# k'v of two batches in spare PSUM columns, ups in halves, w_v in longer runs and a new order of steps, in an attention and channel-mix kernel

## The chip, the cores and the metric

The kernel runs on one core of a Trainium2 chip. The metric is the device time of one execution in microseconds; of several executions the median is given. The core has five engines that run their own instruction streams and wait for each other through semaphores: PE (TensorE, matrix products), DVE (VectorE), ACT (ScalarE), POOL (GpSimd) and SP (SyncE, which here only issues transfers). PE multiplies out of SBUF and writes into PSUM, which has eight banks of 512 fp32 columns on each of 128 partitions. DVE and ACT read PSUM and write SBUF.

## The reference

Eight batches of attention with separate normalisations of q and k, and then a channel mix on its output:

```
q_s = softmax of q over the head dimension;  k_s = softmax of k over the sequence
kv  = k_s^T v   (64 x 64 for each head);      x = q_s kv          # q, k, v: (8, 8, 576, 64)
x:  (8, 8, 576, 64) -> (8, 576, 512)
xk  = mu_k * x + (1 - mu_k) * x_prev;         xr = mu_r * x + (1 - mu_r) * x_prev
out = sigmoid(xr @ w_r) * ((relu(xk @ w_k) ** 2) @ w_v)
```

x_prev is x moved by one position of the sequence, with zeros at the front. The width is 512, the hidden width F is 1024, the sequence 576. Inputs and output are float32; the products are taken in bf16.

## The kernel before, in words

All weights are cast to bf16 and stay in SBUF. The eight batches go through two stages. The attention stage works on halves of a batch (u = 0, 1: four heads each) and leaves the mixed inputs xk and xr of the batch, transposed (512 channels on partitions, 576 positions along the free dimension). The channel-mix stage takes xk by batch and xr by pairs of batches.

**Attention of a half.** `exp` on ACT makes eq and ek out of the loaded q and k. `cast_v` makes vb, whose last column of each head is 1, so that the product with it also gives the column sums. `sum_q` and `scale_q` on DVE normalise q into qs. For the first two batches (NM = 2, the "mixed" ones) `turn_q` transposes qs on PE into a pair of PSUM banks and two `evict_q` copy it to qT, 320 columns from one bank and 256 from the other (in the profile: qT, 128x640 and 128x512 bf16); later batches use a DMA transpose. `kv` is 36 small matmuls, 65 columns wide, into both banks of a pair. After it come, for the later batches, `norm_kv` and `x`, and then the mix from x on ACT and DVE (`shift_x`, `mix_x`). For the two mixed batches `weigh_kv` folds mu into kv instead: for w = 0 (mu_k) a reciprocal and two multiplications, for w = 1 (mu_r) two more, all on DVE, all reading kv in PSUM. Then `x_mixed` takes kvm and qT to xk (w = 0) or xr (w = 1) in two parts, c = 0 (320 positions, 12 matmuls) and c = 1 (256 positions, 8 matmuls), each into its own pair of banks, and `evict_mixed` on ACT or DVE copies each to SBUF.

**Channel mix.** `up(b, f)` is one of the eight tiles of F of one batch: 16 matmuls in two groups (a = 0, 1), 288 positions each, into the two banks of a pair. `relu` on ACT evicts the pair, `square` (DVE or ACT) squares two tiles at once into k2. `gate` (four matmuls), `tanh`, `down` (eight matmuls), `finish` and `store` make 128 rows of output. Gates and downs use single banks.

**PSUM.** Six banks are three pairs, two0 to two2; two are single, one0 and one1. A step that needs a pair takes the one that the plan frees first.

**Order.** `Plan.run` goes through the table ORDER, a list of step numbers with a letter where a step may go to one of several engines (A ACT, D DVE, G POOL). It gives each step a planned start from written costs (`T_NARROW`, `TURN` and the numbers in each `pl.step`), and picks buffers by it. `emit` sorts all steps by planned start and calls them in this order. So ORDER and the costs fix the order of instructions on each engine's queue, and on each queue of transfers, but not the waits: these come from the layer that builds the program, which orders a step behind the steps emitted earlier that touch the same buffers. Every engine runs its queue in order.

**Weights.** w_k comes in two transfers of 1 MB (columns 0 to 511, then 512 to 1023 of F) and is cast in eight steps of 128 columns of F; w_v comes in two transfers of 1 MB, 512 rows each, and is cast in four. Row 128 f + p of w_v lands on partition p, so a partition receives four runs of 2 KB for each transfer.

**Start.** While PE waits in the first microseconds, extra matmuls on an identity (`warm`) are put into planned gaps, up to the start of the step `up(0, 0)`.

In the profile the lines that matter below are L332 (`exp`), L342, L344 and L347 (`sum_q`, `scale_q`), L361 (`turn_q`), L378 (`kv`), L391 and L393 (`weigh_kv`), L410 (`x_mixed`), L454 (`up`), L459 (`relu`), L473 (`gate`), L490 (`down`), L320 (`warm`), and the copies, which all have the line of the helper: L237 on ACT, L238 on DVE and POOL.

Of the kernel before, what the change touches and what calls it, by code (L numbers as in the profile page):

```python
# [20 lines left out]
ORDER = """  # L21
7 0 2 8 1 76 3 80 81 4 9 10 96 11 5 100 78G 77 79A 82 85 83A 12 6 13 84A 97 14 101 86 87 28 102
103A 90 92 91A 104D 93A 98G 99G 19 105 94 95A 16G 88 17G 106 107 108 89A 27 109D 24 110 111A 29
23G 136 15A 114 18D 112 362 363 21G 115D 367 30 113D 31 365 360 22G 25 32 368 26 33 372 20A 37
34 40 366 361 377 375 140 141 116 378 364D 376 370 120 371 369D 121 142 119G 526 536 117 527
143D 138G 122 42 373 118D 537 39G 144D 124D 125 43 137 521 531 123D 139A 44 38G 126 127 130 131A
128 129A 145 146 147 134 41 135A 148 149A 532 150 151D 36G 374A 152 154 153D 385 387 155D 35D
386 382 397 522 379D 156 159 388 523 398 160 389A 158 524 528 380 173 176 177 174 46 161 529 383
381 45 157 390 391 178 530 538 190 539 395 162 132 533 396 163 399A 392 133A 164 393 561 193 166
534 165 384D 47 49 394D 562 541 48 175 167 168 542 169 179 55 180 551 50 546 194 195 552 535 181  # L30
170 547 186 187 172 171 188 182 51 563 183 564 548 556 184 207 412 413 191 192 185 210 417 189
402 418 403 415 410 540 211 241 565 405 209 416 549 411 407 212 208 419D 408 406 244 245 576 196
197 400 56 57 557 571 401 414D 577 213 198 409D 572 200 404D 214 558 199 202 203 201 543 215 559
544 204 206 205 52 216 581 566 582 217 219 53 54 567 220 221 224 218 225 525 222 227 223 568 578
427 432 428 242 550 569 430 243 431 433 420 421 247 226 230 434A 586 246 437 228 248 438 587 579
422 423 58 231 249 254 255 424D 256 59 229 570 583 250 257 560 251 584 545 553 258 253 232 554
61 237 66 252 234 573 574 233 591 64 238 425 606 236 60 426 259 235 63 239 260 435 240 277 261
65 607 452 436 442 447 439D 429D 596 453 262 592 443 440 575 448 275 445 294 450 292 446 278 608
62 279 580 441 295 449D 451 597 293 263 455 264 280 298 598 444A 454A 609 601 299 456 276 265
599 266 600 602 267 268 281 282 270 555 611 612 67 588 269 68 272 621 283 589 271 274 622 273  # L40
285 284 593 73 289 594 69 626 286 610 288 627 457 616 458 603 459A 296 290 287 343 309 460 74
291 467 461 468 462 463 346 465 311 470 472 466 297 312 477 310 313 471 344 75 604 469D 590 628
478 345 473 300 585 314 617 347 71 315 618 302 595 629 316 641 301 305 619 304 464A 306 475 308
646 642 647 630 613 476 307 303 348 474A 317 323 479D 322 349 614 350 620 636 637 319 638 643
324 318 320 485 321 487 488 72 328 644 651 325 652 486 70 497 639 640 498 489D 492 326 329 490
493 327 495 496 482 483 330 491 499D 623 351 332 357 624 661 353 615 653 333 480 356 662 331
494D 481 358 654 352 656 657 631 632 359 484D 334 625 633 340 335 336 355 673 655 339 634 648
337 354 341 517 342 518 338 505 649 666 510 645 650 667 704 671 506 705 511 672 507 681 674 706
707 682 512 635 500 508 509A 513 515 675 676 514D 658 659 677 516 502 501 503 504D 660 519D 668
669 605 670 663 664 665 683 684 678 679 691 685 686 692 696 687 688 697 680 708 520 689 690 701  # L50
702 693 694 703 695 698 699 700
"""


class Plan:
# [6 lines left out]

    TURN = 0.2

# [78 lines left out]
def kernel(  # L143
# [28 lines left out]


    const = ctx.enter_context(tc.tile_pool(name="const", bufs=1))
    psum = ctx.enter_context(tc.tile_pool(name="psum", bufs=1, space=bass.MemoryType.PSUM))
# [110 lines left out]
    def wk_raw():  # L286
        return f32(at("k2", "w"), CT * F).rearrange("p (c a f) -> p a c f", a=2, c=CT)
# [80 lines left out]
    def dma_turn_q(b, u):  # L368
        nc.sync.dma_start_transpose(out=at("qT", b, u)[:],
                                    in_=at("qs", b, u)[:].rearrange("p j c -> p (j c)"))  # L370

    def kv(b, u):
        ps, ek, vb = at("two", "kv", b, u), at("ek", b, u), at("vb", b, u)
        for j in range(J):
            for g in range(2):
                for h in range(2):
                    r = slice(64 * g, 64 * g + 64)
                    nc.tensor.matmul(ps[64 * h:64 * h + 64, g, 0:65],  # L378
                                     lhsT=ek[r, j, 64 * h:64 * h + 64], rhs=vb[r, j, h, :],
                                     start=(j == 0), stop=(j == J - 1))  # L380

    def norm_kv(b, u):
        ps, rz = at("two", "kv", b, u), inv_k(b, u)
        nc.vector.reciprocal(out=rz, in_=ps[:, :, 64])
        nc.vector.tensor_tensor(out=at("kvs", b, u)[:], in0=ps[:, :, 0:64],
                                in1=rz[:, :, None].to_broadcast((128, 2, 64)), op=ALU.mult)

    def weigh_kv(b, u, w):
        ps, rz, rows = at("two", "kv", b, u), inv_k(b, u), slice(2 * w, 2 * w + 2)
        if w == 0:  # L390
# [147 lines left out]

    T_UP, T_GATE, T_DOWN, T_NARROW = 0.98, 0.863, 1.725, 0.5

# [41 lines left out]
    for a in range(2):  # L582
        first.append(dma(2.75, lambda a=a: load_wv(a), uses=[sl("k2", "w")],
                         after=[*queue, *(ev["wk", i] for i in range(FT))]))
# [4 lines left out]
    for b in range(2, B):  # L589
        for u in range(2):  # L590
            for n in "qkv":
                ld(n, b, u, first)

    for n in range(B):
        for u in range(2):
# [26 lines left out]
            s = sl("two", "kv", n, u)  # L622
            p = pl.step("PE", T_NARROW, lambda n=n, u=u: kv(n, u), after=[ke, *vc],
                        uses=[ek, vb, s], lat=0.3, narrow=True)
            if n < NM:
                km = sl("kvm", n, u)
                nk = [p, ev["mu"]]
                for w in range(2):
                    nk.append(pl.step("DVE", 0.75 - 0.2 * w, lambda n=n, u=u, w=w: weigh_kv(n, u, w),
                                      after=nk, uses=[s, km, sl("mub")], lat=0.18))  # L630
                for w in range(2):
                    for c in range(2):
                        s = sl("two", "xm", n, u, w, c)
                        p = pl.step("PE", 0.47 if c == 0 else 0.41,
                                    lambda n=n, u=u, w=w, c=c: x_mixed(n, u, w, c),
# [24 lines left out]
    for b in range(B):  # L660
        mixed = [ev["mix", b, u, 0, c] for u in range(2) for c in range(2)]
        relus = []
        for f in range(FT):
            s, r = sl("two", "up", b, f), sl("rel", b, f // 2)
            ev["up", b, f] = pl.step("PE", T_UP, lambda b=b, f=f: up(b, f),
                                     after=[ev["wk", f], *mixed], uses=[sl("xk", b), s], lat=0.2)
            relus.append(pl.step("ACT", 0.54, lambda b=b, f=f: relu(b, f),
                                 after=[ev["up", b, f]], uses=[s, r], lat=0.2))
            if f % 2:
# [5 lines left out]
    for s in (ev["prep"], ev["up", 0, 0]):  # L675
        pl.link(s, [], [sl("one", "warm")])
    branch = pl.step("PE", 0.3, lambda: part())
    branch["tail"] = "first"
    for i in range(B // 2):
        for m in range(J):  # L680
# [3 lines left out]
                        after=[*ev["wr"], *(ev["mix", b, u, 1, c] for b in bs for u in range(2)  # L684
                                            for c in range(2))],
                        uses=[sl("xr", i), s, th], lat=0.2)
# [146 lines left out]
```

## Time and profile before

| what | value |
|---|---|
| median of 3 runs | 199.26 us (199.06 to 199.76) |
| the profiled execution's own time | 199.28 us |
| its span, first to last instruction | 197.5 us |
| mean granted clock of PE | 0.989 |
| matmuls of up, gate, down (busy) | 66.8, 35.8, 66.2 us |
| DMA | 46.86 MB, mean 237 GB/s over the span |

The span is what the profile's lines cover; about 1.8 us of the time lie around it. In the page, a first part gives the busy time of each engine. A second divides the span into 40 slices of about 4.9 us, with one digit each for the busy tenths; PEclk is the clock that PE was granted, 9 being full. A timeline line gives the start, the time of the group, the engine, the line, the operation, the output and inputs, how many instructions are merged, and in brackets the idle time before it with what ended it. A line of the windows gives a stretch, its length, the busy time (and count) of PE, of PE's weight loads, DVE, ACT and POOL, then PE's granted clock, the DMA's busy share and GB/s.

### The profile page before, as it was taken

The numbers are of one execution on the slowest core, as the hardware profiler recorded it, in microseconds if no ns is written. First come the engines' busy times: TensorE is split into PE (matmuls) and PEld (weight loads), VectorE is DVE, ScalarE is ACT, GpSimd is POOL, SyncE is SP. The second block draws the span as 40 slices with busy tenths as digits, with TensorE's granted clock in tenths as the row PEclk, the third lists the DMA queues.
The fourth block names the chain that finished last, engine by engine and source line by source line (L and its number), as shares of the span: only waits on it lengthen the run. The fifth ranks groups of instructions, "written<-read, shape, count | busy, mean of one in ns | idle before, by whom it ended". The sixth has DMA issues, their size and how long they took to land. (4 is left out here: it accounts for less than half of the span.)

```text
span 197.5 us, 4726 instructions
## 1 busy us (share of the span) xinstructions
PE 186.5 (94%) x1903; PEld 111.4 (56%) x1903; DVE 145.6 (74%) x225; ACT 144.7 (73%) x212; POOL 30.4 (15%) x42
## 2 busy tenths in 40 slices
PE   6699899899999999999998999999999999999991
PEld 4366665655547754664675545755476546664441
DVE  1979896797899799948999779887658859126222
ACT  3898688799797986989769988998749591671210
POOL 2042763420120222000080000230200000000000
PEclk9879999999999999999999999999999999999998
DMA  5999999989999999869993499999622540515634
GB/s 207 371 399 386 389 390 386 389 314 240 276 388 205 229 397 294 272 61 278 403 399 87 86 250 359 318 229 276 236 51 59 113 106 10 124 30 124 162 72 127
DMA packets 35896, 46.86 MB, mean 237 GB/s; under 512 B 16280, under 2 KB 16544, under 8 KB 35872
## 3 DMA queue, kind: packets, MB, share of 16 engines
q1 hardware_dynamic: 35456, 46.02, 77.7%
q10 hardware_dynamic: 416, 0.53, 1.0%
q8 instruction: 15, 0.25, 0.5%
q14 instruction: 9, 0.07, 0.1%
HBM read 33.56 MB, written 9.44 MB: 218 GB/s over the span
## 5 line engine op out<-in xcount | busy, mean ns | idle before, releaser
L454 PE MATMUL two<-xk,wk_bf 128*128 128x288 bf16 x512 | 66.8, 286 | 1.2 <-POOL wk_bf L238 0.9
L490 PE MATMUL one<-wv_bf,k 128*128 128x512 bf16 (+1 forms) x296 | 66.2, 374 | 0.1
L454 PEld LDWEIGHTS <-wk_bf 128*128 128x128 bf16 x512 | 49.8, 98 | 18.1 <-POOL wk_bf L238 1.2
L459 ACT ACTIVATE rel<-two 128x576 bf16<-128x576 f32 x64 | 39.9, 650 | 20.3 <-PE two L454 17.0
L490 PEld LDWEIGHTS <-k 128*128 128x128 bf16 x296 | 28.1, 98 | 31.2 <-issue 0.8
L473 PE MATMUL one<-wr_bf,xr 128*128 128x512 bf16 x144 | 35.8, 379 | 0.0
L238 POOL CAST vb<-ldv 128x1152 bf16<-128x1152 f32 (+1 forms) x17 | 19.2, 1132 | 102.0 <-DMA ldv<-in_v_dram 94.0
L440 ACT ACTIVATE aw<-two,om 128x575 bf16<-128x575 f32 x48 | 32.6, 752 | 2.5 <-PE two L432 2.5
L478 ACT ACTIVATE th<-one 128x512 f32<-128x512 f32 x36 | 21.4, 603 | 13.5 <-PE one L473 13.4
L496 DVE SCALAR_TENSOR_TENSOR ot<-th,one 128x512 f32<-128x512 f32 x33 | 22.4, 681 | 11.9 <-PE one L490 9.1
L469 DVE TENSOR_TENSOR k<-rel 128x1152 bf16<-128x1152 bf16 x22 | 18.6, 860 | 11.3 <-ACT rel L459 11.2
L342 DVE TENSOR_REDUCE rs<-eq 128x18 f32<-128x1152 bf16 x16 | 21.6, 1348 | 3.4 <-ACT eq L332 3.3
L347 DVE TENSOR_TENSOR qs<-eq,inv 128x1152 bf16<-128x1152 bf16 x16 | 23.7, 1484 | 0.3
L445 DVE SCALAR_TENSOR_TENSOR xk<-two,mu,aw 128x576 bf16<-128x576 f32 x24 | 19.1, 812 | 3.3 <-ACT aw L440 3.3
L332 ACT ACTIVATE eq<-ldq 128x1152 bf16<-128x1152 f32 x16 | 18.5, 1170 | 3.2 <-DMA ldq<-in_q_dram 3.0
L473 PEld LDWEIGHTS <-xr 128*128 128x128 bf16 x144 | 13.4, 98 | 13.1 <-issue 0.2
L445 DVE SCALAR_TENSOR_TENSOR xr<-two,mu,aw 128x576 bf16<-128x576 f32 x24 | 19.1, 803 | 1.1 <-ACT aw L440 1.0
L332 ACT ACTIVATE ek<-ldk 128x1152 bf16<-128x1152 f32 x16 | 18.7, 1171 | 0.5 <-DMA ldk<-in_k_dram 0.5
L467 ACT ACTIVATE k<-rel 128x1152 bf16<-128x1152 bf16 x10 | 11.6, 1171 | 0.2
L378 PE MATMUL two<-vb,ek 64*64 64x65 bf16 x576 | 7.9, 197 | 1.0 <-ACT ek L332 0.5
L378 PEld LDWEIGHTS <-ek 64*64 64x64 bf16 x576 | 6.4, 110 | 3.9 <-ACT ek L332 0.9
L320 PE MATMUL one<-ident 128*128 128x256 bf16 x29 | 6.6, 387 | 1.8 <-DVE halves L258 1.8
(56 smaller groups left out, 86.0 us busy)
## 6 DMA issues: line engine op xcount, KB each, us to landing
ldq<-in_q_dram SPq DMA_DIRECT2D x16, 576.0 KB, 5.9
ldk<-in_k_dram SPq DMA_DIRECT2D x16, 576.0 KB, 8.4
out_dram<-ot SPq DMA_DIRECT2D x66, 128.0 KB, 2.5
ldv<-in_v_dram SPq DMA_DIRECT2D x14, 576.0 KB, 7.7
k<-in_moe_w_k_dram SPq DMA_DIRECT2D x2, 1024.0 KB, 12.6
k<-in_moe_w_v_dram SPq DMA_DIRECT2D x2, 1024.0 KB, 11.0
ldv<-in_v_dram SPq DMA_DIRECT2D x4, 288.0 KB, 10.5
xr<-in_moe_w_r_dram SPq DMA_DIRECT2D x1, 1024.0 KB, 13.1
```

The lines of the kernel that those rows point to most:

```text
L238: return {"DVE": nc.vector, "POOL": nc.gpsimd}[eng].tensor_copy(out=out, in_=in_)
L332: nc.scalar.activation(out=at("e" + n, b, u)[:].rearrange("p j (h d) -> p h j d", h=2), in_=at("ld" + n, b, u)[:].rearrange("p h (j d) -> ...
L342: nc.vector.reduce_sum(out=rs[:], in_=at("eq", b, u)[:].rearrange("p j (h d) -> p (j h) d", h=2), axis=AX.X)
L347: nc.vector.tensor_tensor(out=at("qs", b, u)[:].rearrange("p j (h d) -> p (j h) d", h=2), in0=at("eq", b, u)[:].rearrange("p j (h d) -> p ...
L440: nc.scalar.activation(out=at("aw", b, u, h, w)[:, 1:S], in_=x_of(b, u, h)[:, 1:S], func=ACT.Copy, scale=om[:, c:c + 1])
L445: nc.vector.scalar_tensor_tensor(out=blend(b, w)[:, 2 * u + h, :], in0=x_of(b, u, h)[:, 64:64 + S], scalar=mu[:, c:c + 1], in1=at("aw", b, ...
L454: nc.tensor.matmul(ps[:, a, 0:HS], lhsT=wk_bf[:, ct, 128 * f:128 * f + 128], rhs=xk[:, ct, HS * a:HS * a + HS], start=(ct == 0), stop=(ct ...
L459: nc.scalar.activation(out=at("rel", b, f // 2)[:, f % 2, :].rearrange("p (a c) -> p a c", a=2), in_=at("two", "up", b, f)[:, :, 0:HS], fu ...
L473: nc.tensor.matmul(at("one", "rp", i, m)[:], lhsT=at("xr", i)[:, ct, 128 * m:128 * m + 128], rhs=wr_bf[:, ct, :], start=(ct == 0), stop=(c ...
L478: nc.scalar.activation(out=at("th", i, m)[:], in_=at("one", "rp", i, m)[:], func=ACT.Tanh, scale=0.5)
L490: nc.tensor.matmul(at("one", "vp", i, m, a)[:, cols], lhsT=at("k2", i)[:, f, 128 * m:128 * m + 128], rhs=wv_bf[:, f, cols], start=(f == 0) ...
L496: nc.vector.scalar_tensor_tensor(out=at(kept(i, m), i, m)[:, cols], in0=at("th", i, m)[:, cols], scalar=1.0, in1=at("one", "vp", i, m, a)[ ...
```

## The change

The new home of kv for the mixed batches is a third kind of buffer, "spare", which is not new memory: it is columns 320 to 384 of both banks of two1 and two2.

```diff
+    bufs["spare"] = [t[:, :, 320:385] for t in bufs["two"][1:]]
...
+    def kv_of(b, u):
+        if b < NM:
+            return at("spare", "kv", b, u)
+        return at("two", "kv", b, u)[:, :, 0:65]
...
-        ps, ek, vb = at("two", "kv", b, u), at("ek", b, u), at("vb", b, u)
+        ps, ek, vb = kv_of(b, u), at("ek", b, u), at("vb", b, u)
```

`norm_kv` and `weigh_kv` read through `kv_of` as well, and the plan takes a "spare" for these kv instead of a pair. Because `x` writes across columns 320 to 384 of a pair, it gets the weighings of the mixed batches as predecessors in the plan:

```diff
+                weighed += nk[2:]
...
-            p = pl.step("PE", T_NARROW, lambda n=n, u=u: x(n, u), after=[nk, *T],
+            p = pl.step("PE", T_NARROW, lambda n=n, u=u: x(n, u), after=[nk, *T, *weighed],
```

The ups of the two mixed batches become two steps each, one for each group of eight matmuls; the first half needs only the c = 0 parts of xk. A gate needs only the parts of xr whose positions it reads.

```diff
-    def up(b, f):
+    def up(b, f, parts=(0, 1)):
...
-        for a in range(2):
+        for a in parts:
...
+            for a in ((0, 1),) if b >= NM else ((0,), (1,)):
+                ev["up", b, f] = pl.step(
+                    "PE", T_UP * len(a) / 2, lambda b=b, f=f, a=a: up(b, f, a),
+                    after=[ev["wk", f], *(ev["mix", b, u, 0, c] for u in range(2)
+                                          for c in range(2) if c in a or c == 0 or b >= NM)],
+                    uses=[sl("xk", b), s], lat=0.2)
```

w_v is read so that partition p gets rows 4p to 4p + 3 of each half, one run of 8 KB. The order of F within a half changes with it, and the casts of w_k follow: each takes every fourth column of its half, a read stride of four fp32.

```diff
-            ap=[[C, 128], [128 * C, 4], [1, C]]))
+            ap=[[4 * C, 128], [1, 4 * C]]))
...
-        a, c = f // 4, 128 * (f % 4)
-        copy(eng, wk_bf[:, :, 128 * f:128 * f + 128], wk_raw()[:, a, :, c:c + 128])
+        units = wk_raw()[:, f // 4, :, :].rearrange("p c (e i) -> p c i e", i=4)
+        copy(eng, wk_bf[:, :, 128 * f:128 * f + 128], units[:, :, f % 4, :])
```

Written costs change (T_NARROW 0.5 to 0.55, TURN 0.2 to 0.25, `x_mixed` 0.47 and 0.41 to 0.52 and 0.44, a transfer of w_v 2.75 to 2.5), and ORDER is a new table with 16 more steps. At the start the new order on PE is: turn_q of half 0 (two1), kv of half 0 (two1's spare), turn_q of half 1 (two2), x_mixed of half 0 for xk (c = 0 on two0, c = 1 on two1), kv of half 1 (two2's spare), x_mixed of half 0 for xr (two2, two1), x_mixed of half 1 (two0, two2, two1), the first ups, and among these the last x_mixed of half 1. In the old order kv of half 0 takes two2, turn_q of half 1 and kv of half 1 take two0, and all x_mixed of batch 0 come ahead of the first up. For batch 1, too, the last x_mixed moves from ahead of the ups to behind the first of them. The first transfers on SP keep their order up to the k of batch 1; then the two halves of a v are swapped, and the loads of batch 2 have another order.

More of the change, by code (lines that the diff above doesn't have):

```diff
@@ L21 @@
 ORDER = """
[L22 to L51, printed above, removed]
+7 8 9 0 2 10 11 1 76 3 80 96 81 4 12 13 5 6 14 100 101 77 28 82 78A 84A 79G 83A 98G 19 97 99G 85
@@ new lines @@
+86 102 87 103D 27 88 90 104D 18G 91A 105 106 107 17D 92 94 15G 16G 89A 24 108 93A 95A 20G 109A
+23G 29 30 110 26 111D 112 113A 360 361 364 31 362 114 115D 363 33 371 370 136 140 367 368 22A
+372 365 385 21D 369 32 384 374 378 37 377 386 116 366D 375 381 379 141 142 376 120 382 143D 373A
+121 25 552 34 117 118D 542 383 380D 553 122 40 543 119G 125 124D 126 547 537 123A 138G 130 137
+131A 139D 39G 127 128 129A 145 144D 146 134 135A 132 133A 148 147 150 149A 151D 152 387D 538 395
+42 396 153D 413 36A 412 397 43 409 405 41 406 414 35G 410 398 156 38G 548 159 544 411 415D 407
@@ new lines @@
+173 399 400 158 389 160 176 46 391 44 392 45 157 403 393 388 545 161 390 554 177 175 402 404 555
+154 162 401D 178 49 190 539 155D 163 408D 549 164 174 394A 165 179 540 557 166 47 550 541 51 193
+558 168 180 577 578 169 562 567 167 563 170 48 568 181 579 546 187 194 182 171 209 186 172 580
+188 183 191 564 572 55 184 189 428 185 207 416 417 54 418 50 195 556 210 565 429 192 196 197 419
+241 423 420D 551 424 431 432 211 573 212 592 433 566 421 57 243 426 587 244 208 434 422 427 425D
+56 430D 58 593 198 213 245 588 199 214 200 202 201 574 204 559 435A 203 575 52 215 216 226 597
@@ new lines @@
+560 561 576 53 205 206 598 217 582 583 584 219 221 594 220 218 222 246 258 446 224 448 223 453
+595 449 443 227 447 581 607 228 242 247 229 585 454 436 444 225 61 450D 65 437 602 248 608 230
+249 569 231 603 251 63 570 254 250 438 255 252 599 253 257 439 232 60 66 600 589 440A 233 256
+234 237 235 59 596 238 451 236 622 452 275 239 240 623 441 64 442 445A 455D 261 458 471 472 612
+463 571 62 294 456 293 590 464 613 617 461 459 457 278 74 262 279 263 260 259 466 277 591 462
+292 276 618 460A 280 298 264 265 295 299 624 625 468 467 469 614 465D 266 267 281 586 615 470D
@@ new lines @@
+268 627 604 628 282 270 271 272 637 269 605 69 283 67 638 626 619 273 274 289 285 606 473 620
+284 287 286 288 632 474 309 633 68 609 75 73 290 493 475D 478 310 291 479 296 476 345 71 477 312
+313 72 494 483 610 642 297 486 480D 601 343 484 311 481 482 488 644 487 344 489 346 315 643 347
+300 301 634 645 302 621 657 316 306 611 635 485D 491 647 305 658 616 308 303 307 304 327 629 349
+492 495D 314 648 490A 317 322 646 652 653 636 319 70 318 630 659 654 323 660 661 324 325 639 655
+320 662 511 350 508 321 512 501 503 326 502 348 506 640 329 330 504 507 513 667 509 514 663 328
@@ L52 @@
+510D 332 351 668 687 353 333 669 515D 331 352 354 688 357 355 498 356 359 656 496 641 499 670
+671 672 497 677 505D 334 500D 673 689 678 336 335 337 340 664 690 358 339 341 679 342 691 665
+533 680 526 534 682 531 527 528 532 338 683 516 517 692 720 518 535A 721 681 519 520A 697 698
+722 723 521 693 523 674 529 530D 675 649 666 522 650 524 631 684 685 651 525A 694 699 676 686
+695 702 700 703 707 708 696 712 713 701 724 704 536 705 706 709 717 710 714 711 718 719 715 716
 """
 class Plan:
-    TURN = 0.2
+    TURN = 0.25
@@ L382, in norm_kv @@
     def norm_kv(b, u):
-        ps, rz = at("two", "kv", b, u), inv_k(b, u)
+        ps, rz = kv_of(b, u), inv_k(b, u)
         nc.vector.reciprocal(out=rz, in_=ps[:, :, 64])
@@ L388, in weigh_kv @@
     def weigh_kv(b, u, w):
-        ps, rz, rows = at("two", "kv", b, u), inv_k(b, u), slice(2 * w, 2 * w + 2)
+        ps, rz, rows = kv_of(b, u), inv_k(b, u), slice(2 * w, 2 * w + 2)
         if w == 0:
@@ L537 @@
     ev: dict = {}
-    T_UP, T_GATE, T_DOWN, T_NARROW = 0.98, 0.863, 1.725, 0.5
+    T_UP, T_GATE, T_DOWN, T_NARROW = 0.98, 0.863, 1.725, 0.55
     def dma(cost, fn, after=(), uses=(), lat=2.0):
@@ L582 @@
     for a in range(2):
-        first.append(dma(2.75, lambda a=a: load_wv(a), uses=[sl("k2", "w")],
+        first.append(dma(2.5, lambda a=a: load_wv(a), uses=[sl("k2", "w")],
                          after=[*queue, *(ev["wk", i] for i in range(FT))]))
@@ L592 @@
                 ld(n, b, u, first)
+    weighed: list = []
     for n in range(B):
@@ L621 @@
                              uses=[qs, qT], lat=3.3)]
-            s = sl("two", "kv", n, u)
+            s = sl("spare" if n < NM else "two", "kv", n, u)
             p = pl.step("PE", T_NARROW, lambda n=n, u=u: kv(n, u), after=[ke, *vc],
@@ L633 @@
                         s = sl("two", "xm", n, u, w, c)
-                        p = pl.step("PE", 0.47 if c == 0 else 0.41,
+                        p = pl.step("PE", 0.52 if c == 0 else 0.44,
                                     lambda n=n, u=u, w=w, c=c: x_mixed(n, u, w, c),
@@ L660 @@
     for b in range(B):
-        mixed = [ev["mix", b, u, 0, c] for u in range(2) for c in range(2)]
         relus = []
         for f in range(FT):
-            s, r = sl("two", "up", b, f), sl("rel", b, f // 2)
-            ev["up", b, f] = pl.step("PE", T_UP, lambda b=b, f=f: up(b, f),
-                                     after=[ev["wk", f], *mixed], uses=[sl("xk", b), s], lat=0.2)
+            s, r, both = sl("two", "up", b, f), sl("rel", b, f // 2), []
+            for a in ((0, 1),) if b >= NM else ((0,), (1,)):
[4 more added lines that the diff above has]
+                    uses=[sl("xk", b), s], lat=0.2)
+                both.append(ev["up", b, f])
             relus.append(pl.step("ACT", 0.54, lambda b=b, f=f: relu(b, f),
-                                 after=[ev["up", b, f]], uses=[s, r], lat=0.2))
+                                 after=both, uses=[s, r], lat=0.2))
             if f % 2:
@@ L676, with needs @@
         pl.link(s, [], [sl("one", "warm")])
+    def needs(b, m, c):
+        lo, n = PARTS[c]
+        return b >= NM or any(lo <= blk - J * (b % 2) < lo + n for blk in (2 * m, 2 * m + 1))
     branch = pl.step("PE", 0.3, lambda: part())
@@ L684 @@
                         after=[*ev["wr"], *(ev["mix", b, u, 1, c] for b in bs for u in range(2)
-                                            for c in range(2))],
+                                            for c in range(2) if needs(b, m, c))],
                         uses=[sl("xr", i), s, th], lat=0.2)
```

## The prediction

> **What bounds it now.** I read the page first, then the waits of PE, then the timeline of the first 40 us, then the windows of PE's clock.
>
> ```profile
> span 197.5 us, 4726 instructions
> ...
> PE 186.5 (94%) x1903; PEld 111.4 (56%) x1903; DVE 145.6 (74%) x225; ACT 144.7 (73%) x212; POOL 30.4 (15%) x42
> ...
> PE   6699899899999999999998999999999999999991
> ...
> PEclk9879999999999999999999999999999999999998
> ```
>
> PE is busy 94% of the span and full from 40 us to the last gates; it is short of work only in the first 36 us. So a change gains or loses where PE starves early, and every us by which PE's steady work starts later is a us at the end: nothing behind it has slack to give back. The waits of PE are small: the longest in the steady part is 0.51 us at 108 us (for ACT's exp of k), and one of 0.89 us lies in the first ups.
>
> ```profile
> 10.84 1.17 ACT L237 COPY qT<-two 128x640 bf16<-128x640 bf16 x2
> ...
> 11.38 0.71 PE L378 MATMUL two<-vb,ek 64*64 64x65 bf16 x36
> 11.89 1.18 ACT L332 ACTIVATE ek<-ldk 128x1152 bf16<-128x1152 f32 x1
> ...
> 12.16 0.17 DVE L391 RECIPROCAL inv<-two 128x2 f32<-128x2 f32 x1
> ...
> 12.37 1.13 DVE L393 SCALAR_TENSOR_TENSOR kvm<-two,inv,mub 128x128 bf16<-128x128 f32 x4
> ...
> 14.29 0.48 PE L378 MATMUL two<-vb,ek 64*64 64x65 bf16 x36 [0.28 <-ACT xk L237]
> ...
> 16.77 0.59 ACT L237 CAST xk<-two 128x512 bf16<-128x512 f32 x1 [0.42 <-PE two L410]
> ...
> 17.48 1.17 ACT L332 ACTIVATE eq<-ldq 128x1152 bf16<-128x1152 f32 x1
> ...
> 17.56 4.09 PE L454 MATMUL two<-xk,wk_bf 128*128 128x288 bf16 x32
> ...
> 22.54 4.09 PE L454 MATMUL two<-xk,wk_bf 128*128 128x288 bf16 x32 [0.89 <-POOL wk_bf L238]
> ...
> 35.64 4.08 PE L454 MATMUL two<-xk,wk_bf 128*128 128x288 bf16 x32 [0.34 <-DVE xk L238]
> ```
>
> Two marks follow: the first up of batch 0 at 17.56, the first of batch 1 at 35.64; from there PE is never short by more than those 0.51 us. The row at 14.29 is what the change aims at: the second kv waits 0.28 us for a pair of banks.
>
> ```profile
> 5.27:8.68 3.41, 1.90 (x9) 0.97 (x8) 3.12 (x4) 2.88 (x6) 0.00 (x0) 1.00 1.01 356
> 8.68:12.09 3.41, 3.06 (x52) 2.34 (x52) 3.34 (x6) 3.00 (x5) 0.66 (x1) 0.51 1.03 400
> ...
> 32.57:35.98 3.41, 2.52 (x65) 1.63 (x54) 2.38 (x7) 3.11 (x6) 2.02 (x2) 1.00 1.06 391
> ```
>
> The second figure is PE's busy time, the last but two the granted clock. After a stretch with 1.90 of 3.41 us busy the next 3.41 us ran at half clock; after one with 2.52 the clock stayed full (36 to 40 us).
>
> **What the change costs, part by part.** The new home of kv is columns 320 to 384 of both banks of pairs two1 and two2, which also take the transposed q, the mixed x and the ups. The built program gives for every instruction what it waits for, and there kv and its readers are ordered against every other engine's access to the same pair, though the columns differ. So kv is not freed from the pairs: it is tied to two of them while others use them, and the weighing that reads it too. The trace of before cannot show this; I follow the chain with its durations. A wait ends about 0.07 us after its releaser (DVE's first weighing of 32.97 ends at 33.31, PE's weight load starts at 33.38; kv ends 14.77, DVE starts 14.83), and on ACT and DVE an instruction starts up to 0.1 before the recorded end of the last.
>
> Start. ACT's cast of v ends 10.94 as before; the copy of the 512 columns of qT (0.59) ends 11.43; kv of half 0 waits for it and runs 11.50 to 12.21 (0.71). The copy of the 640 columns (0.69) now waits for kv: 12.27 to 12.96. Behind it on ACT is exp of the second k (1.18): to 14.04, before 13.07. DVE's reciprocal waits for that copy too: 13.02; the four weighings (1.13, the first 0.34, then 0.26 each) end at 13.57, 13.83, 14.09, 14.36, before 13.50 the last. x_mixed of w 0, c 0 on two0 starts 13.64; w 0, c 1 on two1 waits for the fourth weighing: 14.43 to 14.84 (8 matmuls 0.41). DVE copies qT of half 1 (640 columns, 0.48) to 14.76; kv of half 1 (spare of two2) waits for that copy: 14.84 to 15.32; the other copy (0.42) waits for kv: 15.38 to 15.80. Reciprocal 0.17, two weighings 15.93 to 16.53; x_mixed of half 0, w 1, c 0, on two2, waits for them: 16.60 to 17.1; its eviction on ACT (640 columns, 0.69): 17.16 to 17.85; only then the other two weighings, 17.91 to 18.51; the next x_mixed pair (20 matmuls, 0.69) 18.58 to 19.27. First up 19.3: 1.75 later, with one x_mixed still to do.
>
> Batch 0. Four ups (4.09) and that x_mixed (0.41) end at 23.8. Here the 0.89 us wait goes, since the second half of w_k is cast before (landed 20.19, two POOL casts of 1.14: 22.5). Four more ups and a transpose (0.55): 28.4; two gates (0.86 each): 30.1, before 28.7. Meanwhile relu of the first up ends 21.02, exp of q (1.17), queued behind it on ACT, 22.1, before 18.65; DVE's sum starts 22.15, before 18.70. Its chain (1.35, 0.27, cast 0.43, square 0.76, scale 1.64) ends 26.45; the next sum waits for its exp at 26.56; 1.35, 0.27, copy 0.48, scale 1.36: 29.95, before 28.19, so just in time for PE's second transpose, 30.1 to 30.65 (before 28.70).
>
> Batch 1. kv of half 0 30.7 to 31.15, two gates to 32.9, x_mixed 32.95 to 33.85. DVE casts the last half of v (0.74) between the weighings, to 33.8, and kv of half 1 runs 33.87 to 34.35 (before 32.21). Then two2 again takes turns: eviction of half 0 (0.69) after kv, to 35.10; reciprocal and two weighings to 35.95; x_mixed to 36.3; the other two weighings to 36.96; eviction to 37.71. First up of batch 1: 37.78 against 35.64, 2.14 later. One x_mixed of batch 1, done before this mark in the old order, comes behind it: 0.41.
>
> Clock. Between 15.3 and 18.9 PE has about 1.5 us of work (0.69, 0.36 and the first 0.4 of the next pair), below the 1.90 after which the clock halved. The next 3.41 us at half clock hold the first ups and lose at most 1.7 us; where the stretches fall against the work differs, so I take 1.0, with 0 and 1.7 as ends. [...]
>
> The rest. Ups in halves issue the same 16 instructions: 0. The strided read in the casts of w_k has no row: at least as now (0.43 on DVE), at most like the 1024-element cast of w_v there, 1.05. I take 0.43, as the same size; two of the casts on DVE are on the chain, so up to 0.6 more; POOL's are covered by PE's lateness, 1.3 us. w_v in longer runs: its transfers may land 0.5 us sooner or not at all; POOL waits for them at 33.6 and 36.3, PE uses them at 39.4, so 0. x waiting for all weighings: over by 37, x comes after 45: 0. The swapped loads on SP (halves of v, k of batch 2) land ahead of their users, which come later now: 0. The new table behind 40 us: PE has the same steps and 21 runs of narrow matmuls in both orders; the wait of 0.51 may vanish or stay, I take -0.25.
>
> Sum against the profiled execution, 199.28 (span 197.5), which stands 0.02 above the median of 199.26: 199.28 + 2.14 + 0.41 - 0.25 + 1.0 = 202.6.
>
> **Rivals.** The clock stays full: 201.6. For it: the only half-clock stretch came after a pause of 1.5 us, and here the longest is 1.3. Against: by busy time the stretch is emptier.
>
> A second half-clock stretch, once batch 1's ups begin: between 34.4 and 37.8 PE has about 1.9 us of work, between the 1.90 that halved it and the 2.52 that did not. PE is full behind it, so all 1.7 us count: 204.3.
>
> Not slower: the delay of the start is swallowed. Before, batch 1 waits for its own loads (v lands at 30.22, used 32.21) and the 0.89 us wait vanishes; if DVE's and ACT's chain of batch 1 keeps its old places, its first up comes by 35.9 and the time is 199.28 + 0.41 - 0.25 = 199.4. It decides at DVE's sum of q of batch 1: at 20 or sooner instead of 22.15. Against it: the exp that feeds it stands behind the relu of the first up on ACT.
>
> That the change does what it says, so that kv runs beside the other users of a pair: then the wait of 0.28 at 14.29 goes, but PE still meets the second half of w_k at 22.5, so only the 0.25 of 108 us is left: 199.28 - 0.25 = 199.0, and less if batch 1 gains too. The waits in the built program speak against it. [...]
>
> **How the numbers follow.** Forecast, pair waits with one half-clock stretch: 0.42, its own range 202.0 to 203.4 (the clock's loss from 0.4 to 1.7). Clock full: 0.25. Two stretches: 0.22. Swallowed: 0.05, within 0.3% (0.6 us, about what a measurement here can tell from no change). As meant: 0.02, faster by more. The last 0.04 is for waits behind 40 us that I did not follow, over 204.6. The range 201.0 to 204.6 holds the first three but for their tails. Slower: 0.93.
>
> **What would show it.** In the new trace ACT's two copies of the first qT should lie on both sides of kv, with the last at about 12.3; the first up at 19.3; DVE's sum of q of batch 1 at 22 to 23; the first up of batch 1 at 37.8, or near 38.8 with the clock; no POOL wait in batch 0's ups; a dip of PEclk in slice 4 or 5. I am wrong if the first up comes before 18.3, if batch 1's comes before 36.5, or if PE starves behind 40 us by more than 0.6 us in all.

## The result and the profile after

| | before | after |
|---|---|---|
| median | 199.25 us (198.63 to 199.76, 6 runs) | 205.74 us (205.05 to 209.67, 6 runs) |
| span of the profiled execution | 197.5 us | 203.9 us |
| first up of batch 0, of batch 1 | 17.56, 35.64 | 23.12, 43.45 |
| DVE's last `finish` starts at | 193.47 | 200.24 |

After/before is 1.0324 (95% interval 1.0286 to 1.0361): 6.5 us slower. One of the six executions of after, 209.67, ran in a slower state and is left out of the ratio; the other five lie between 205.05 and 206.78. The direction and the chain behind the pairs of banks came as predicted, the size did not: 205.74 lies above the range of 201.0 to 204.6.

The page of after, the same lines as shown of before:

```profile
span 203.9 us, 4719 instructions
...
PE 190.2 (93%) x1903; PEld 113.1 (55%) x1903; DVE 141.8 (70%) x225; ACT 146.3 (72%) x212; POOL 33.0 (16%) x42
...
PE   6993499979999999999999999999999999999992
...
PEclk9999589999999999999999999999999999999999
```

PE is as full as before from 40 us on. What is new lies in slices 3 and 4 (counted from 0; 15 to 25 us), where PE is busy a third to a half of the time, and in slice 4 the clock is halved. The timeline of after there, in order of time:

```profile
11.18 0.71 PE L388 MATMUL two<-vb,ek 64*64 64x65 bf16 x36
...
11.96 0.69 ACT L242 COPY qT<-two 128x640 bf16<-128x640 bf16 x1 [0.84 <-PE two L388]
...
12.69 0.17 DVE L401 RECIPROCAL inv<-two 128x2 f32<-128x2 f32 x1 [0.30 <-ACT qT L242]
...
14.56 0.48 PE L388 MATMUL two<-vb,ek 64*64 64x65 bf16 x36
...
16.30 0.96 PE L420 MATMUL two<-qT,kvm 64*64 64x320 bf16 x32 [1.04 <-DVE kvm L403]
...
17.55 0.61 DVE L403 SCALAR_TENSOR_TENSOR kvm<-two,inv,mub 128x128 bf16<-128x128 f32 x2 [1.30 <-ACT xr L242]
18.21 0.69 PE L420 MATMUL two<-qT,kvm 64*64 64x256 bf16 x20 [0.95 <-DVE kvm L403]
...
20.52 5.66 POOL L243 CAST wk_bf<-k 128x512 bf16<-128x512 f32 x5 [6.98 <-DMA k<-in_moe_w_k_dram]
...
23.12 3.06 PE L464 MATMUL two<-xk,wk_bf 128*128 128x288 bf16 x12 [4.01 <-POOL wk_bf L243]
...
43.45 4.57 PE L464 MATMUL two<-xk,wk_bf 128*128 128x288 bf16 x36 [0.32 <-ACT xk L242]
```

The first seven lines are the predicted chain: the copy of 640 columns waits for kv, the reciprocal for that copy, the later weighings for an eviction of x_mixed from the same pair. The eighth is the surprise. POOL starts the casts of w_k at 20.52, and PE, which has done its x_mixed at 18.9, stands for 4.01 us, until the second of these casts has ended (23.06). In the timeline of before the same casts came in two groups:

```profile
16.00 1.17 POOL L238 CAST wk_bf<-k 128x512 bf16<-128x512 f32 x2 [2.01 <-DMA k<-in_moe_w_k_dram]
20.19 3.41 POOL L238 CAST wk_bf<-k 128x512 bf16<-128x512 f32 x3 [3.02 <-DMA k<-in_moe_w_k_dram]
```

The first two, at 16.00, needed only the first transfer of w_k; the second landed at 20.19. In after all of them wait for the second. Raw w_k lies in SBUF as (row tile c, half a of F, column), so a view of half a that runs over all four row tiles also spans the columns of the other half between them. The contiguous views of before did so too, and their casts waited for one transfer only; with a step inside the view, the layer that inserts the waits makes each cast wait for both. That the layout is the cause is shown by experiment 2; that the layer takes a view with a step by its whole span is inferred from it. DVE's first cast comes at 20.49, at the same event.

The rows by form show a second cost, the cast itself. First after:

```profile
L243 POOL CAST wk_bf<-k 128x512 bf16<-128x512 f32 x5 | 5.7, 1171 | 7.0 <-DMA k<-in_moe_w_k_dram 7.0
L243 DVE CAST wk_bf<-k 128x512 bf16<-128x512 f32 x2 | 1.1, 569 | 2.3 <-DMA k<-in_moe_w_k_dram 2.3
L242 ACT CAST wk_bf<-k 128x512 bf16<-128x512 f32 x1 | 1.1, 1123 | 0.0
```

and then the same rows of a kernel that is after with the old contiguous casts (the first experiment):

```profile
L243 POOL CAST wk_bf<-k 128x512 bf16<-128x512 f32 x5 | 2.9, 613 | 5.2 <-DMA k<-in_moe_w_k_dram 5.2
L243 DVE CAST wk_bf<-k 128x512 bf16<-128x512 f32 x2 | 0.8, 392 | 0.0
L242 ACT CAST wk_bf<-k 128x512 bf16<-128x512 f32 x1 | 0.6, 608 | 0.0
```

The figure after the comma is the mean in ns: 1.8 to 1.9 times as long on ACT and POOL, 1.45 times on DVE, for the same bytes read in steps of 16 bytes. POOL's mean holds a first cast of 1.52 us beside one on DVE; the other four took 1.07 to 1.09. And the windows of after, stretches of 3.41 us laid against its changes of the recorded clock (20.20 and 27.02), show what PE's pauses go with (second figure PE's busy time, last but two the granted clock):

```profile
16.79:20.20 3.41, 1.38 (x41) 0.86 (x33) 0.61 (x2) 2.47 (x4) 0.00 (x0) 1.00 1.05 388
20.20:23.61 3.41, 0.49 (x3) 0.32 (x4) 1.21 (x2) 0.00 (x0) 3.09 (x3) 0.50 1.05 390
23.61:27.02 3.41, 3.41 (x21) 1.77 (x20) 0.14 (x1) 1.76 (x3) 3.41 (x4) 0.50 1.05 390
```

The clock was halved from 20.20 to 27.02. So the first 12 matmuls of up took 3.06 us where the same 12 took 1.63 in the kernel with contiguous casts.

### The profile page after: what moved, and what is told of

Read it like the earlier page. It is cut to its first block, busy times and chain, and to the rows that moved or that the text cites. A ratio compares the mean times of both kernels' runs of the same rounds, so it can differ in the third digit from the quotient of the medians.

```text
span 203.9 us, 4719 instructions
## 1 busy us (share of the span) xinstructions
PE 190.2 (93%) x1903; PEld 113.1 (55%) x1903; DVE 141.8 (70%) x225; ACT 146.3 (72%) x212; POOL 33.0 (16%) x42
## 3 DMA queue, kind: packets, MB, share of 16 engines
HBM read 33.56 MB, written 9.44 MB: 211 GB/s over the span
## 5 line engine op out<-in xcount | busy, mean ns | idle before, releaser
L464 PE MATMUL two<-xk,wk_bf 128*128 128x288 bf16 x512 | 68.9, 290 | 4.4 <-POOL wk_bf L243 4.0
L243 POOL CAST vb<-ldv 128x1152 bf16<-128x1152 f32 (+1 forms) x17 | 20.4, 1217 | 93.7 <-DMA ldv<-in_v_dram 77.7
L347 DVE TENSOR_REDUCE rs<-eq 128x18 f32<-128x1152 bf16 x16 | 21.6, 1347 | 4.8 <-ACT eq L337 4.8
L352 DVE TENSOR_TENSOR qs<-eq,inv 128x1152 bf16<-128x1152 bf16 x16 | 22.8, 1429 | 1.5 <-DMA qT<-qs 1.4
L479 DVE TENSOR_TENSOR k<-rel 128x1152 bf16<-128x1152 bf16 x22 | 17.0, 774 | 5.5 <-ACT rel L469 5.4
L455 DVE SCALAR_TENSOR_TENSOR xr<-two,mu,aw 128x576 bf16<-128x576 f32 x24 | 19.3, 810 | 0.7 <-ACT aw L450 0.7
L420 PE MATMUL two<-qT,kvm 64*64 64x256 bf16 (+2 forms) x160 | 6.7, 271 | 3.2 <-DVE kvm L403 2.8
L325 PE MATMUL one<-ident 128*128 128x256 bf16 x29 | 7.1, 408 | 1.8 <-DVE halves L263 1.8
```

Source lines behind the costliest of these rows:

```text
L243: return {"DVE": nc.vector, "POOL": nc.gpsimd}[eng].tensor_copy(out=out, in_=in_)
L347: nc.vector.reduce_sum(out=rs[:], in_=at("eq", b, u)[:].rearrange("p j (h d) -> p (j h) d", h=2), axis=AX.X)
L352: nc.vector.tensor_tensor(out=at("qs", b, u)[:].rearrange("p j (h d) -> p (j h) d", h=2), in0=at("eq", b, u)[:].rearrange("p j (h d) -> p ...
L455: nc.vector.scalar_tensor_tensor(out=blend(b, w)[:, 2 * u + h, :], in0=x_of(b, u, h)[:, 64:64 + S], scalar=mu[:, c:c + 1], in1=at("aw", b, ...
L464: nc.tensor.matmul(ps[:, a, 0:HS], lhsT=wk_bf[:, ct, 128 * f:128 * f + 128], rhs=xk[:, ct, HS * a:HS * a + HS], start=(ct == 0), stop=(ct ...
```

## The experiments

The times of before stood at 199.1 to 199.5 us in every comparison. Marks are the start of the first up of batch 0, of batch 1, and of the last `finish`, from each profile:

| kernel | median us | ratio to before (95%) | batch 0 | batch 1 | last finish |
|---|---|---|---|---|---|
| before | 199.25 | | 17.56 | 35.64 | 193.47 |
| after | 205.74 | 1.0324 (1.0286 to 1.0361) | 23.12 | 43.45 | 200.24 |
| 1 contiguous casts | 200.51 | 1.0063 (1.0023 to 1.0102) | 18.88 | 37.40 | 193.92 |
| 2 halves apart | 202.32 | 1.0159 (1.0100 to 1.0218) | 19.21 | 39.52 | 196.04 |
| 3 before, units only | 204.40 | 1.0247 (1.0199 to 1.0295) | 22.20 | 41.38 | 198.61 |
| 4 before, spare only | 200.44 | 1.0053 (1.0024 to 1.0081) | 19.36 | 36.52 | 194.70 |
| 5 single banks | 198.38 | 0.9955 (0.9925 to 0.9984) | 17.19 | 36.06 | 192.71 |
| 6 contiguous, filled pauses | 199.84 | 1.0032 (1.0007 to 1.0058) | 18.80 | 37.33 | 193.84 |
| 7 after, filled pauses | 205.02 | 1.0267 (1.0206 to 1.0327) | 24.28 | 44.22 | 200.81 |
| 8 single banks, units | 206.44 | 1.0348 (1.0291 to 1.0405) | 23.41 | 43.54 | 201.39 |
| 9 single banks, units, halves apart | 199.48 | 1.0025 (0.9994 to 1.0056) | 18.29 | 36.95 | 193.46 |

**1. Contiguous casts.** After without the new units of F: w_v is read as before and the casts of w_k take contiguous columns. The spare columns, the ups in halves and the new table stay.

```diff
-            ap=[[4 * C, 128], [1, 4 * C]]))
+            ap=[[C, 128], [128 * C, 4], [1, C]]))
...
-        units = wk_raw()[:, f // 4, :, :].rearrange("p c (e i) -> p c i e", i=4)
-        copy(eng, wk_bf[:, :, 128 * f:128 * f + 128], units[:, :, f % 4, :])
+        a, c = f // 4, 128 * (f % 4)
+        copy(eng, wk_bf[:, :, 128 * f:128 * f + 128], wk_raw()[:, a, :, c:c + 128])
```

> The changed kernel with the order of F, the reading of w_v and the casts of w_k put back; spare columns, half ups and the new table stay. Theory: the changed kernel lost most of its time to the casts of w_k, whose first half waited for both transfers (20.5 us instead of 16.0) and which then ran slower; with them put back the casts start at 16.0 again, the first up comes at 18.9 to 19.3, batch 1's first up at 37 to 38, and the time is 201.0 to 202.5 us. Rival: the waits for the pairs and the new table cost nearly all, and this stays at 204 us or more.

200.51 us, half a us below the range expected (the gain later in the kernel, told below): 5.2 of the 6.5 us lost are the units. The first ups stand at 18.88 and 37.40, some 0.4 us before my prediction for the pair waits (19.3 and 37.78):

```profile
18.88 1.63 PE L464 MATMUL two<-xk,wk_bf 128*128 128x288 bf16 x12
```

No pause for w_k is left on this line of the timeline. The ten times lie in two groups, 199.1 to 199.7 and 201.3 to 201.7; experiment 6 asks whether PE's clock parts them. All marks of experiment 1 come from an execution of the lower group (199.40), so what they say of the cost holds for that group. Against it the units cost 6.3 us (205.73 in the profiled execution of after), against the median 5.2.

**2. Halves apart.** After, with raw w_k laid out half by half, so that the strided view of one half touches nothing of the other. The casts keep their step of 16 bytes.

```diff
-        return f32(at("k2", "w"), CT * F).rearrange("p (c a f) -> p a c f", a=2, c=CT)
+        return f32(at("k2", "w"), CT * F).rearrange("p (a c f) -> p a c f", a=2, c=CT)
```

> The changed kernel with the raw w_k laid out so that each half is one closed region (half outermost, then the four row tiles); the strided casts and the 8 KB runs stay. Theory (the wait for the other half is the main cost): the casts of the first half start at 16.0, the first up at 18.9 to 19.3, and the time is within 0.7 us of the kernel with the old units, 201 to 203 us. Rival (the slower strided casts, 1.13 us each on POOL against 0.59, are the main cost): the ups keep waiting for casts and the time is 203.5 to 205 us.

202.32 us: the wait for the second transfer is worth 3.4 of the 5.2 us, and its cause is shown, since the layout alone took it away. With four times from 201.5 to 203.5 the split into 3.4 and 1.8 is good to about 1.4 us (an estimate from the intervals of the table). POOL's casts now start when the first half lands, but still take 1.1 us each in place of 0.61 (timeline):

```profile
15.58 3.17 POOL L243 CAST wk_bf<-k 128x512 bf16<-128x512 f32 x3 [2.02 <-DMA k<-in_moe_w_k_dram]
```

The other 1.8 us are more than the 0.7 that I allowed. The two profiled executions, 201.52 here and 199.40 in experiment 1, show where such a difference arises. The first up comes only 0.33 later, and no wait for a cast stands ahead of it, but here the clock was halved from 17.66 to 21.07 (windows):

```profile
14.25:17.66 3.41, 1.66 (x69) 1.35 (x69) 1.52 (x6) 2.30 (x5) 2.08 (x3) 1.00 1.05 390
17.66:21.07 3.41, 3.16 (x29) 2.10 (x30) 2.17 (x3) 1.33 (x3) 1.89 (x3) 0.50 1.05 389
```

The x_mixed ahead of the first up took 1.18 us in place of 0.69 and the first 12 matmuls of up 2.55 in place of 1.63, so that the x_mixed among the ups starts 1.25 late (21.69 against 20.44). Another 0.88 comes by the next transpose of q (28.85 against 26.72), which waits for DVE's scale; ahead of that, DVE's second cast took 1.40 us in place of 0.36 and its square 1.60 in place of 0.76. So more than half of the difference between these two executions came with the clock and the rest behind slower steps on DVE.

**3. Before, units only.** Before with the new read of w_v and the strided casts, nothing else.

> The kernel before with the new order of F, 8 KB runs of w_v and strided casts of w_k alone; its own table, kv in pairs. Theory: its casts wait for both halves of w_k as well, the first up comes at 21.7 to 22.2 instead of 17.6, PE's clock halves in the pause of 4 us, and the time is 202.5 to 204.5 us. Rival: the pause is taken up by the wait of 0.89 us and by the slack before batch 1, and it is under 201 us.

204.40 us, as expected, and 5.2 above before. So the units cost the same, within what the intervals can tell, with and without the other edits. The same two lines as in after, now in the old order (timeline of this kernel):

```profile
20.62 5.81 POOL L238 CAST wk_bf<-k 128x512 bf16<-128x512 f32 x4 [6.90 <-DMA k<-in_moe_w_k_dram]
...
22.20 5.22 PE L454 MATMUL two<-xk,wk_bf 128*128 128x288 bf16 x21 [4.83 <-POOL wk_bf L238]
```

**4. Before, spare only.** Before with kv of the mixed batches in the spare columns of two1 and two2 (the first diff of the change), with the old table and the old units.

> The kernel before with kv of the two mixed batches in the spare columns alone; its own table, whole ups, old units. Theory (kv is tied to two pairs and waits for their other users): the copies of the first transposed q stand on both sides of kv, the first up comes at 19.5 to 20 instead of 17.6, and the time is 200.8 to 202.5 us, more by up to 1.7 if PE's clock halves. Rival (kv is freed from the pairs): the first up comes at 17.6 or sooner and the time is 198.7 to 199.3 us.

200.44 us, 1.25 above before; a little less than expected, with the marks 1.8 and 0.9 late. So moving kv into spare columns costs time by itself. PE waits three times, 2.1 us in all, for the weighings; the list of PE's waits in before has none for them.

**5. Single banks.** Experiment 1 with kv of batch 0 in one0 and one1 instead of the spare columns: for each head pair g one bank, nothing of a pair. The reciprocal becomes two, and three filling matmuls are left out, since they would use the same bank.

```diff
+        if b == 0 and "general" not in st:
+            return [bufs["one"][1 - g][:, 256 * u:256 * u + 65] for g in range(2)]
+        ps = at("spare", "kv", b, u) if b < NM else at("two", "kv", b, u)[:, :, 0:65]
+        return [ps[:, g, :] for g in range(2)]
```

> The changed kernel with the old units, and kv of batch 0 in spare columns of the two single banks, which nobody else needs before the first gate (one bank for each half of the rows, two reciprocals instead of one; three filling matmuls of PE left out, which would write there); kv of batch 1 stays in the pairs. Theory (kv in a pair waits for its other users and makes them wait): the two copies of the first transposed q stand together again, the first up comes at 17.1 to 17.6 instead of 18.9, batch 1's first up at 35.9 to 36.6 instead of 37.4, and the time is 197.9 to 198.8 us. Rival (the new table is late for other reasons): the first up stays behind 18.4 and the time at 199.4 us or more.

198.38 us, as expected: 2.1 below the median of experiment 1 (1.2 between the profiled executions, 198.20 and 199.40), and 0.45% below before (interval 0.9925 to 0.9984), the only version here that beats it. What the change aimed at, kv out of the way of the pairs, does gain once kv of batch 0 really shares no pair with the others. Single banks on before's own table, without the ups in halves and the new order, were not run. The last x_mixed ahead of the ups and the first up now follow each other without a wait (timeline):

```profile
14.52 2.54 PE L428 MATMUL two<-qT,kvm 64*64 64x320 bf16 x52
17.19 1.63 PE L472 MATMUL two<-xk,wk_bf 128*128 128x288 bf16 x12
```

**6 and 7. Filled pauses.** Extra matmuls on the identity go into the pauses ahead of the ups, 7 and 7 in the kernel of experiment 1, and 7, 7 and 16 in after, to see whether PE's clock then stays full. They compute nothing that is used.

```diff
+        for _ in range({(0, 0, 1, 0): 7, (0, 1, 0, 1): 7}.get((b, u, w, c), 0)):
+            warm()
```

> The changed kernel with the old units and 14 more filling matmuls on PE (seven ahead of x_mixed of half 0 for xr, seven ahead of x_mixed of half 1, the two pauses of 1 us at 15.2 and 17.2). Theory of the clock: without them the times fall into two groups, 199.1 to 199.7 and 201.3 to 201.7 us, because in some executions PE's clock halves after these pauses; with them all executions are at 199.1 to 199.9. Rival (the groups have another cause, or the filling delays PE): the upper group stays, or all times move up by 0.3 us or more.

> The changed kernel as it is with the same 14 filling matmuls and 16 more ahead of the first up, in the pause of 4 us in which PE waits for the casts of w_k. Theory of the clock: the first ups run at full clock, about 2 us are saved at the first ups, and the time is 203.3 to 204.3 us. Rival (the casts, not the clock, set the pace of batch 0's ups): 205 us or more.

Experiment 6: 199.84 us, with one of twelve times above 201, where experiment 1 had five of ten; but half of the twelve lie above the 199.9 that I expected of all. The clock alone does not make the upper group of experiment 1: one stretch of 3.41 us at half clock takes 0.0085 off the mean clock of such an execution (an estimate: half of 3.41 us in 200 us), and the one of 201.5 us has a mean of 0.996, so it had none, while one of 199.45 has 0.988. What makes the two groups stays open. Experiment 7 is a miss: 205.02 us, two times near 203.8 and two near 206.2. In its profile, taken of the execution of 206.29 us, the fill ended at 21 us, the casts of w_k started only at 21.6 (20.5 in after), PE stood still until 24.28 for POOL's, and the clock was halved from 24 to 27 us. It tells nothing on what the clock costs in after.

**8 and 9. Single banks with the units.** Experiment 5 with the strided casts and the long runs of w_v put back (8), and the same with the halves of raw w_k apart (9).

> after with kv of batch 0 in the single banks (as in the version that took the strided casts and the long w_v runs out, which took 198.38). Theory: the casts of w_k set the first up by themselves, so what is done to kv ahead of them is hidden. Casts of the first half start again at 20.5, first up again at 23.0 to 23.3, time 204.8 to 206.3, so no gain against after's 205.7, though the same edit gained 2.1 without the strided casts. Rival, the two losses simply add: first up about 21, time 203.2 to 204.0.

> The kernel of the run before with raw w_k laid out half by half, so that the first casts wait for one transfer: what is left of the units is the read in steps of 16 bytes (and w_v in long runs). Theory: with kv out of the way PE is ready at 17.2, POOL's casts start at 16 and take 1.1 us in place of 0.6, so now the slower casts are bare on the path, in batch 0 and behind it: first up 17.5 to 18.3, time 199.8 to 201.2, 1.4 to 2.8 above the version without the strided casts (198.38). Rival: the 1.8 us that the strided casts cost beside the pair waits came from the clock there, and they cost nothing by themselves: first up 17.2, time 198.0 to 199.0.

Experiment 8: 206.44 us, 0.1 above the range expected and no gain against after, though the same edit gained 2.1 us without the units (by the medians). The losses do not add: where the casts of w_k come late, what is done to kv ahead of them is hidden. PE waits longer for the same event (timeline):

```profile
23.41 3.06 PE L472 MATMUL two<-xk,wk_bf 128*128 128x288 bf16 x12 [5.98 <-POOL wk_bf L243]
```

Experiment 9: 199.48 us, 1.1 above experiment 5 (1.4 by their ratios to before) and 7 us below experiment 8, which differs by one line of layout. The forecast was 199.8 to 201.2, so a little too high. The slow cast is now bare on the path:

```profile
18.29 1.71 PE L472 MATMUL two<-xk,wk_bf 128*128 128x288 bf16 x12 [0.58 <-POOL wk_bf L243]
```

This up is 1.10 us later than in experiment 5. Of that, 0.65 was there before any cast of w_k: ACT's exp of the second q, which waits for its load, starts at 6.96 against 6.31, and everything behind it is as much later. The wait for the cast adds the other 0.45 (0.58 us between x_mixed and up, where experiment 5 has 0.13).

Long runs of w_v brought nothing that shows, though no run has them without the strided casts. POOL's first cast of w_v starts at 33.51 in experiment 9 and at 33.56 in experiment 5, which has the short runs, and PE waits for w_v in neither. That a transfer lands 5.9 us after issue in after (median) and 11.0 in before goes with the later issue (29.73 against 23.63): issued at 23.46 in experiment 9, long runs took 11.1.

## Why the prediction was wrong, step by step

**The chain of the pair waits: right.** Predicted starts in batch 0 were 11.50 (kv), 13.02 (reciprocal), 14.84 (second kv), 16.60 and 18.58 (x_mixed); measured in after 11.18, 12.69, 14.56, 16.30 and 18.21, each about 0.3 earlier, since ACT's first copy of qT started at 10.51 and not at 10.84. With the units taken out (experiment 1) the first ups come 1.32 and 1.76 after before's, predicted 1.75 and 2.14. The mechanism stands: other columns of a pair are no home of their own, because the waits go by the pair (by its tile or by its banks; no run here parts these).

**The casts of w_k: the step that failed.** I wrote that "the 0.89 us wait goes, since the second half of w_k is cast before" and costed the strided read at nothing, "as the same size", with "POOL's are covered by PE's lateness, 1.3 us". This term, 0 with 0.6 as its upper end, measured 5.2 us by the medians (205.74 against 200.51; 204.40 against 199.19). Two things were missed. The casts of the first half wait for both transfers, 20.5 in place of 16.0 us: worth 3.4 us beside the pair waits (experiment 2) and 7.0 without them (8 against 9). I had taken the waits of kv from the built program, where this wait stands too, and did not look at those of the casts. And each cast is up to twice as long. Beside the pair waits that left 1.8 us, in the profile more than half of it with the clock; with kv out of the way a wait of 0.58 us stands on the path. (The 1.14 that I counted for a contiguous cast on POOL was the mean of three, which took 0.61, 1.74 and 1.17.)

My reading of what covers the cast was right as far as it went: with the halves apart and the pair waits left in, the first up was only 0.33 late. But a cover of 1.3 us does not hide 4.5.

**The clock, +1.0: came, larger, and where it falls is a draw.** The half clock fell on the first ups of after, 3.06 us for 12 matmuls in place of 1.63, so 1.4. In before, after and experiment 2 the clock stayed halved for 3.41 us or twice that (8.68 to 12.09, 20.20 to 27.02, 17.66 to 21.07), and these steps lie otherwise against the work each time: one stands at 20.20 in after, at 17.66 in experiment 2. The fall went with the busy time of the stretch just ended, on which I put the term: it came behind 1.38 us in after, 1.66 in experiment 2, 1.90 in before, 2.10 in experiment 5 and 2.25 in experiment 9, and the clock stayed full behind 2.10 in experiment 9, 2.24 in after and in experiment 1, and 2.52 in before. From 2.10 to 2.25 both happened; what decides there stays open. With the same pauses, which I had foreseen, the stretches of experiment 1 had 2.24 and 2.46 us busy and the clock stayed full; one of experiment 2 had 1.66 and it fell. In after it fell behind 1.38 us, and behind the pause that I had not foreseen, with 0.49 us busy in the next stretch, it stayed halved over the ups, to 27.02. So 1.0 was a guess at where the stretches would lie. The length of the pause, on which the rival "clock full" rested, does not part the cases: when the clock fell PE had stood for 1.14 us in before (7.54 to 8.68), 1.09 in after (19.11 to 20.20) and 0.70 in experiment 2 (16.96 to 17.66), while in experiment 1 it stayed full through pauses of 1.04 and 0.95.

**Behind batch 1's first up, +0.16 in my sum (0.41 for a moved x_mixed, less 0.25): wrong sign.** From that mark to the last finish the old table takes 157.83 us, after 156.79, experiment 1 156.52. The 0.41 was a misreading, which the section on the change shares: in before, 12 matmuls of x_mixed already ran behind the first up of batch 1, and in after 8 do. PE's idle time behind the mark falls from 0.82 us to 0.29 (0.19 in experiment 1), so the wait of 0.51 at 108 us went whole and not by half. The other 0.5 to 0.7 us, less busy time for the same work but four matmuls, I could not place. In the profile of experiment 1 this gain takes back most of the 1.76 by which the pair waits are late at the mark: 0.45 is left at the last `finish`. Its median stands 1.3 above before's all the same, since half of its executions are 2 us longer.

**The sum as measured.** By the medians, units +5.2 and all the rest +1.3. By the marks of the three profiled executions, pair waits +1.76, units with their clock +6.05 (43.45 against 37.40), work behind the mark −1.04: 6.77 at the last `finish`. The two ways differ because the profile of experiment 1 is of its lower group. Of the rivals, "clock full" (201.6) is the nearest to the change without its units, 200.5. "As meant" fell in the form that was built, and experiment 5 shows what it would have taken.

## What to carry to other kernels

When a view gets a stride, look in the built program at what each of its readers now waits for: a strided view that spans other data can wait for that data too, and the cure may be one line of layout (206.44 to 199.48 us). Columns borrowed inside a pair of banks bring that pair's waits with them: kv in spare columns cost 1.25 us on its own, and with kv of batch 0 in banks of its own the kernel beat the one before. Price a loss behind the event that comes last: a gain of 2.1 us ahead of a late transfer was worth nothing until the transfer was no longer waited for. And ask which executions a profile stands for before its marks are set against a median: experiment 1's median lay between two groups of times.

## What the hardware showed that I had not expected

A cast of f32 to bf16, 128x512, that reads in steps of 16 bytes took 1.10 to 1.16 us on ACT, where a contiguous one took 0.60 to 0.62. I had counted on no difference. On POOL most strided casts took 1.07 to 1.12 and most contiguous ones 0.61 or 0.62; on DVE most took 0.53 to 0.61 and 0.36 to 0.48. The exceptions are as large as the stride: in before two contiguous casts on POOL took 1.74 and 1.17 while DVE did its scale and its square, and in experiment 2 the two strided casts on DVE took 1.46 and 1.40 while POOL was casting. Whether POOL and DVE slowed each other there no run tests. By the means the step cost ACT about 0.5 us a cast, POOL 0.55 and DVE 0.13 to 0.18 (experiment 1 against after, 5 against 9); what in it costs the time was not shown.
